# Sparse attention with a soft mixture behind it: the last tile's product in four parts, no filling products, the last copies and late loads in another order

## The chip, the cores and the metric

The kernel runs on one core of one Trainium2 chip. What counts is the device time of one execution in microseconds (us); the table below gives the median, the lowest and the highest of three runs of the kernel before, and the time of the one execution that was profiled.

## The reference

Two stages follow each other. The first is block-sparse attention: 4 batches, 8 heads, 768 positions, 64 columns per head, in blocks of 32 positions (24 blocks). A query block sees itself, its two neighbours, the first and the last block, and three sampled blocks; the first and last query blocks see everything. The second is a soft mixture of 8 experts with 4 slots each.

```python
def _attn_ref(q, k, v, sampled_blocks):
    scores = scale * np.matmul(q, k.transpose(0, 1, 3, 2))
    mask = np.abs(blk_i - blk_j) <= window
    mask = mask | (blk_i == 0) | (blk_j == 0) | (blk_i == n_blocks - 1) | (blk_j == n_blocks - 1)
    ...                                   # and the sampled blocks of each query block
    scores = np.where(mask, scores, -1000000000.0)
    attn = np.exp(scores - np.max(scores, axis=-1, keepdims=True))
    attn = attn / (np.sum(attn, axis=-1, keepdims=True) + 1e-09)
    return np.matmul(attn, v)

def _moe_ref(x, phi, w1, w2):             # x: 3072 x 512, phi: 512 x 32
    logits = x @ phi
    d = softmax of logits over the 3072 rows
    slot_input = (d.T @ x).reshape(E, S_per_e, D)
    for e in range(E):                    # w1[e]: 512 x 1024, w2[e]: 1024 x 512
        slot_out[e] = np.maximum(slot_input[e] @ w1[e], 0.0) @ w2[e]
    c = softmax of logits over the 32 slots
    return c @ slot_out.reshape(n_slots, D)
```

Everything is in float32. The softmax over all 3072 rows means that no expert can start before the last attention tile is done.

## The kernel before, in words

The attention is cut into 24 tiles of 128 rows, 6 per batch, named here (batch, tile): the last one is (3,5). A tile holds two units of two query blocks each, and heads come in two halves, r = 0 and 1. For a unit, PE forms the scores (`s`, line 538) from staged keys (`kst`), DVE takes their maxima (`nm`), ACT the exponentials (`p`), and DVE transposes them (`ptt`). POOL copies the value rows of the sampled blocks into staging buffers (`vrs`, line 482; six buffers, so that a buffer comes free when an older tile's product has read it). The product with the values (`av`, line 630, in `av_heads`) is 44 matrix products per half r of a tile, 42 for the last tile, which touches the border; PE runs each float32 product as two instructions and as many weight loads. DVE divides by the sums (`rs`, `x`, from `av_out`).

Four tiles make a group (`plan_group`). PE transposes each tile's `x` (`mxt`, line 826), ACT or DVE copies the result out (`xT`, line 375 or 377 in `evac`), PE forms the logits of the four tiles (`ml`, line 862); then come maximum (`nmx`), exponential (`dT`), a transposition (`md`, copied to `d`) and the sums `ms` = d.T @ x (line 917), which DVE adds to `sacc` and `ssum` (line 926). The last group, gi = 5, holds tiles (3,2) to (3,5). Its last tile is "split": half r = 0 goes to two banks of its own and is transposed before half r = 1 is done. Behind the last group stands a short serial stretch (`mr`, `mc`, `selw`, `psS`, `sT`), and then the experts: `pf` (line 1285, first weights) and `pso` (line 1293, second weights), which run over 64 weight pieces of 512 KB, and at last the combination (`po`, line 1388), copied out and stored.

The order of the work is not written out: each step is added to a plan with the engines that may do it, an estimated duration, what it depends on, the buffers that it takes, and a key. `Plan.run` simulates this with its own estimates and emits the instructions of every engine in the order that comes out. The key decides among steps that could start at about the same time; where a step may go to two engines, the simulation picks one. The engines then run their instructions in that fixed order and wait for each other by semaphores.

`Plan.run` also puts in filling products: where its simulation sees PE idle for more than 0.45 us late in the attention, it emits a few 128x128 products on the identity (`st`, by `warm`, line 397) whose result nobody reads.

SP issues the loads of weights. The first 23 pieces are loaded during the attention; then come 20 "late" ones in the order of `LORD`: digits are fresh buffers, "k" the freed key buffer (`kw`), "v" the freed value buffer `v1`, "o" two of the buffers that held transposed exponentials (`wx`). SP waits for each buffer in this order. The remaining 21 pieces go into buffers that the experts' products have read.

Of the kernel before, what the change touches and what calls it, by code (L numbers as in the profile page):

```python
# [21 lines left out]
P = 128  # L22
# [32 lines left out]

LORD = [0, 1, "k", "k", "k", 2, 3, 4, 5, "o", "o", "v", "v", "v", "v", 6, 7, 8, "v", "v"]
H1, HALF = 3, 4
# [24 lines left out]
class Plan:  # L82
# [14 lines left out]
    def run(self):  # L97
# [81 lines left out]
        todo = {e: [t for t in order if t.eng == e and t.pre] for e in at}  # L179
        pe_end = 0.0  # L180
        pe = []
        for t in order:
            q = todo[t.eng]
            while q and q[0].start <= t.start + 1.6:
                u = q.pop(0)
                u.vals = u.pre(u.eng)
            if t.eng == "PE":

                if (self.fill[0].fin < t.start < self.fill[2].fin and t.start - pe_end > 0.45
                        and sum(p == "s" and a < t.start and z > pe_end for p, _, a, z in spans) < SB):  # L190
                    self.fill[1](int((t.start - pe_end - 0.15) / 0.28))
                pe_end = t.fin
            i = t.f(t)
            if t.eng == "PE":
                last = next(i for i in reversed(self.tc.nc.cur_bb.bb.instructions) if i.engine == E_.PE)
                pe.append((t.fin, last.name))
            elif t.pace:

                name = [n for f, n in pe if f <= t.start - 1.5][-1]
                self.tc.add_manual_dep(i.ins, name, mybir.DependencyInfo(  # L200
                    mybir.DependencyClass.Sync, mybir.DependencyReason.DATA), reason="pace")
# [3 lines left out]
def attn_moe_kernel(ctx, tc, qT, kT, vfull, vtab, sampled, phi, w1, w2, out):  # L205
# [431 lines left out]

    def av_heads(T, rs_):

        vt, us = vtile[T.b], T.units  # L640
        one = len(us) == 1
        m = 64 * len(us)
        for n, c in enumerate((4, 5)):
            for r in rs_:
                for g, s_ in G2:
                    av_mm(T.av, 64 * r if one else 0, m, g, r, T.pt[r][s_, c, 0:m // BLK].rearrange("p j q -> p (j q)"),
                          vt[s_, :, VPOS((0, NB - 1)[n]), r, :], n == 0, False)
        for c in (1, 2):
            for w, u in enumerate(us):
                for r in rs_:  # L650
                    for g, s_ in G2:
                        av_mm(T.av, 64 * r if one else 64 * w, 64, g, r,
                              T.pt[r][s_, c, 2 * w:2 * w + 2].rearrange("p j q -> p (j q)"),
                              vt[s_, :, VPOS(2 * u.g + c), r, :], False, False)
        for n in range(NR + 1):
            for w, u in enumerate(us):
                for r in rs_:
                    for j in range(2):
# [14 lines left out]
    def plan_av(T, n):  # L673
# [12 lines left out]
        else:  # L686

            T.split = T is tiles.get((B - 1, NT - 1))

            def heads(t, r):  # L690
                if T.split and r == 0:
                    T.av = T.av0 = [psA.tile([P, 512], F32, tag="s", name="av", bufs=SB) for g in range(2)]
                elif r == 0 or T.split:
                    new_av(T)
                av_heads(T, (r,))
            if T.split:
                t_0 = add(lambda t: heads(t, 0), ("PE", 2.16), deps, n + 0.5, acq=[("s", use)] * 2, kind="av", mode="W3", ni=176)
                last = []
                t_a = add(lambda t: heads(t, 1), ("PE", 2.25), [t_0], n + 0.5, acq=[("av", last)], kind="av", mode="W3", ni=176)
                T.out = [add(lambda t, r=r: av_out(T, T.av if r else T.av0, 0, P, slice(r, r + 1)), ("DVE", 0.8 if r else 1.0),  # L700
# [115 lines left out]
    def plan_group(gi, Ts, last, final=False):  # L816
        st = Rec()
        t_xT, xT_use = [], []
        for n, T in Ts:
# [13 lines left out]
            if split:  # L833
                for h in range(2):
                    t_t = add(lambda t, h=h, turn=turn: turn(t, cs=range(h, 4, 2)), ("PE", 0.27), [T.out[h]], n + 2 + 0.01 * h, mode="F", ni=4,
                              acq=[] if h else [("pt", b_use)])
                    t_o = add(lambda t, h=h, out=out: out(t, cs=slice(h, 4, 2)), ("ACT", 0.4), [t_t], n + 2.1 + 0.01 * h,
                              acq=[] if h else [("xT", x_use)])
# [6 lines left out]
            t_t = add(turn, ("PE", 0.3), T.out, n + 2, acq=[("pt", b_use)], kind="xt", mode="F", ni=8)  # L845
            t_o = add(out, [("DVE", 0.69), ("ACT", 0.59)], [t_t], n + 2.1, acq=[("xT", x_use)], kind="xto")
            T.x_use.append(t_t)
# [111 lines left out]
        if split:  # L959
            t_lt.deps.append(t_dt)  # L960
            state.t_f = t_f = add(factor, ("ACT", 0.3), [t_do], k + 0.31)
            state.t_lo = t_lo
        use[2].append(t_do)
        t_s = add(sums, ("PE", 0.4), [t_do], k + 0.6, acq=[("pt", use[3])], kind="sum", mode="C", ni=16)
        d_use.append(t_s)
        state.t_s = t_s
        for _, T in Ts:
            T.x_use.append(t_s)
# [96 lines left out]
    for gi in range(6):  # L1065
        Ts = done[4 * gi:4 * gi + 4]
        t_m, k = plan_group(gi, Ts, Ts[-1][0])

# [94 lines left out]
    lp_use.extend([t_end, t_5])  # L1163
    t_z = add(f_zero, ("POOL", 1.1), [state.t_acc0.deps[0]], k, acq=[("xT", [t_end]), ("x", [t_end])])
    t_7 = [add(f_out, (e, 0.4), [t_end, t_z], k + 1.1) for e in ("DVE", "ACT")]
# [25 lines left out]
    ms.__enter__()  # L1191
    plan.fill = max(qks.items())[1], lambda n: warm(None, n), tiles[B - 1, NT - 1].t_av
    with tc.manual_schedule(engines={E_.SP}):
# [292 lines left out]
```

## Time and profile before

| | us |
|---|---|
| median of 3 runs | 309.68 |
| lowest and highest | 306.84 to 310.25 |
| the profiled execution, its own time | 307.04 |
| the span of its trace | 305.2 |
| around the span | 1.84 |
| attention until the first `pf` product | 252.0 |
| experts, combination, stores | 53.2 |

All places below are in us from the start of the span. The profiled execution is 2.64 us shorter than the median of the three runs. A trace shows for every instruction when it started and how long it took; where an engine stood idle in front of one, the releaser is named, or "issue" where it waited for nothing that the profile shows.

### The profile page before, as it was taken

Reading aid. Unit: us, or ns where it says so; the run is one execution under the profiler, and the core shown is the slowest. Engines: PE = TensorE matmul, PEld = TensorE weight load, DVE = VectorE, ACT = ScalarE, POOL = GpSimd, SP = SyncE. Lnnn points to the kernel's source line nnn. Section 1 sums busy time; section 2 is a strip of 40 time slices with the busy share of each in tenths; the row PEclk is TensorE's granted clock in tenths of the full one; section 3 lists DMA queues with packets and bytes.
Section 4 is the critical chain, followed back from the end, with each engine's and each line's share of the span. In section 5 each row is a group of like instructions: output and inputs, shape, how many; then the busy total and the mean of one; then the engine's idle time right before and its main releaser. Section 6 shows DMA issues by size and latency. Waiting matters only on the chain.

```text
span 305.2 us, 17541 instructions
## 1 busy us (share of the span) xinstructions
PE 275.6 (90%) x7147; PEld 191.6 (63%) x7147; DVE 219.3 (72%) x504; ACT 165.5 (54%) x522; POOL 177.4 (58%) x484
## 2 busy tenths in 40 slices
PE   7698999989999989999998999999797889999950
PEld 6158677666877765777675777767564652455640
DVE  4788988777999898898999689988882336012360
ACT  0877876842877584487577737676720041202450
POOL 2668788878758998394889759478454214000000
PEclk9869999999999999999999999999978899999996
DMA  7935676574576465264654625686686399999997
GB/s 244 400 116 160 177 198 193 143 203 102 165 207 182 132 170 139 64 171 120 170 151 127 175 55 154 154 222 178 212 258 227 107 382 375 413 410 406 313 305 256
DMA packets 31634, 63.61 MB, mean 208 GB/s; under 512 B 5313, under 2 KB 18754, under 8 KB 31554
## 3 DMA queue, kind: packets, MB, share of 16 engines
q1 hardware_dynamic: 31408, 62.37, 65.0%
q8 instruction: 56, 0.92, 1.3%
q14 instruction: 24, 0.20, 0.3%
q10 hardware_dynamic: 146, 0.13, 0.1%
HBM read 56.19 MB, written 6.29 MB: 205 GB/s over the span
## 4 chain that ended last, share of the span: by engine, by line
PE 70%; DVE 6%; DMA 5%; issue 4%; ACT 4%; POOL 4%; SPq 2%; POOLq 2%; ACTq 1%; DVEq 0%
PE av L630 28%; PE s L538 11%; PE avd L630 6%; PE pf L1285 5%; PE pso L1293 4%; PE mxt L826 4%; PE sd L735 3%; PE ms L917 2%; PE po L1388 2%; DMA ktile<-in_kT_dram 2%; PE ml L862 2%; POOL vrs L482 1%; POOLq L363 1%; ACT kst L464 1%; POOL kst L458 1%
## 5 line engine op out<-in xcount | busy, mean ns | idle before, releaser
L482 POOL COPY vrs<-v 128x260 f32 x264 | 95.7, 405 | 33.7 <-PE av L630 21.5
L558 ACT ACTIVATE p<-s,nm 128x256 f32<-128x256 f32 x176 | 72.6, 474 | 21.5 <-DVE nm L553 17.5
L630 PE MATMUL av<-v,ptt 64*64 64x130 f32 (+2 forms) x1728 | 76.1, 289 | 0.8 <-DVE x L625 0.6
L630 PEld LDWEIGHTS av<-v,ptt 64*64 64x64 f32 (+2 forms) x1728 | 51.3, 134 | 26.4 <-issue 15.0
L565 DVE STREAM_TRANSPOSE ptt<-p 128x512 f32<-128x512 f32 x88 | 58.6, 689 | 2.1 <-ACT p L558 2.0
L553 DVE TENSOR_REDUCE nm<-s 128x2 f32<-128x512 f32 x88 | 55.6, 676 | 2.3 <-PE s L538 2.0
L538 PE MATMUL s<-kst,q 64*32 64x256 f32 x1408 | 50.4, 387 | 4.7 <-ACT pd L766 2.8
L458 POOL COPY kst<-ktile 128x384 f32<-128x384 f32 x88 | 42.9, 507 | 13.3 <-PE s L538 13.3
L464 ACT ACTIVATE kst<-ktile 128x128 f32 x204 | 45.7, 300 | 8.7 <-PE s L538 5.7
L630 PE MATMUL av<-vrs,ptt 64*32 64x130 f32 x2112 | 45.8, 276 | 2.8 <-issue 2.8
L538 PEld LDWEIGHTS s<-kst,q 64*32 64x32 f32 x1408 | 30.0, 107 | 17.1 <-issue 4.1
L630 PEld LDWEIGHTS av<-vrs,ptt 64*32 64x32 f32 x2112 | 35.6, 105 | 4.2 <-issue 4.0
L766 ACT ACTIVATE pd<-sd,nb 128x384 f32<-128x384 f32 x32 | 16.6, 578 | 14.9 <-DVE nb L761 14.3
L375 ACT COPY xT<-mxt 128x512 f32<-128x512 f32 (+1 forms) x14 | 7.8, 555 | 30.1 <-PE mxt L826 29.7
L630 PE MATMUL avd<-v,ptd 64*64 64x130 f32 x768 | 23.1, 271 | 1.1 <-DVE x L625 0.9
L630 PEld LDWEIGHTS avd<-v,ptd 64*64 64x64 f32 x768 | 21.7, 132 | 2.6 <-PE s L538 1.3
L501 POOL TENSOR_SCALAR q<-q 128x256 f32<-128x256 f32 x33 | 13.2, 405 | 11.6 <-DMA q<-in_qT_dram 9.5
L753 DVE TENSOR_REDUCE nm<-sd 128x1 f32<-128x384 f32 x32 | 16.4, 545 | 3.7 <-PE sd L735 3.7
L735 PE MATMUL sd<-ktile,q 64*32 64x384 f32 x256 | 18.1, 531 | 1.0 <-ACT p L558 0.7
L770 DVE STREAM_TRANSPOSE ptd<-pd 128x384 f32<-128x384 f32 x32 | 16.3, 552 | 2.1 <-ACT pd L766 2.0
L625 DVE TENSOR_TENSOR x<-av,rs 128x512 f32<-128x512 f32 (+2 forms) x28 | 16.9, 605 | 1.1
L826 PE MATMUL mxt<-ident,x 128*128 128x128 f32 x96 | 16.1, 288 | 1.1 <-ACT lst L890 1.1
(128 smaller groups left out, 268.8 us busy)
## 6 DMA issues: line engine op xcount, KB each, us to landing
w<-in_w_dram SPq DMA_DIRECT2D x18, 512.0 KB, 8.1
v<-in_w_dram SPq DMA_DIRECT2D x12, 512.0 KB, 10.2
q<-in_qT_dram SPq DMA_DIRECT2D x47, 128.0 KB, 2.7
w<-in_w_dram SPq DMA_DIRECT2D x44, 128.0 KB, 3.5
out_dram<-ob SPq DMA_DIRECT2D x19, 256.0 KB, 3.2
ktile<-in_kT_dram SPq DMA_DIRECT2D x48, 96.0 KB, 3.0
v<-in_w_dram SPq DMA_DIRECT2D x24, 128.0 KB, 3.4
kw<-in_w_dram SPq DMA_DIRECT2D x6, 512.0 KB, 6.6
```

What stands on the lines that cost most here:

```text
L458: POOL.tensor_copy(out=st[:, :, w:w + 96], in_=kv[:, :, (i - 1) * BLK:(i + 2) * BLK])
L464: ACT.activation(out=st[:, :, o:o + BLK], in_=src, func=AF.Copy, scale=1.0)
L482: POOL.tensor_copy(out=st[:, :, j:j + 1, :], in_=vf[:, :, ds(t.vals[j], 1), :])
L538: PE.matmul(u.s[r][32 * p:32 * p + 32, j, :], lhsT=u.q[s_, p, j, :], rhs=kd[j][0][s_, p, :], start=True, stop=True)
L553: DVE.tensor_reduce(out=u.nm[r], in_=u.s[r], axis=AX.X, op=ALU.max, negate=True)
L558: ACT.activation(out=u.p[r][:, j, :], in_=u.s[r][:, j, :], func=AF.Exp, bias=u.nm[r][:, j:j + 1], scale=1.0)
L565: DVE.transpose(out=T.pt[r][:, :, 2 * w:2 * w + 2, :].rearrange("p k j q -> p j k q"), in_=u.p[r].rearrange("p j (k q) -> p j k q", k=8))
L625: DVE.tensor_tensor(out=x, in0=a[:, :, :, 0:D], in1=rs[lo:hi].unsqueeze(3).to_broadcast([hi - lo, 2, 2 * n, D]), op=ALU.mult)
L630: PE.matmul(av[:, r * 2 * D1:(r + 1) * 2 * D1].rearrange("p (a d) -> p a d", a=2), lhsT=lhsT, rhs=rhs, start=start, stop=stop)
L735: PE.matmul(u.s[r][k][32 * p:32 * p + 32, :], lhsT=T.dq.q[s_, p, j, :], rhs=kt[s_, p, 384 * k:384 * (k + 1)], start=True, stop=True)
L766: ACT.activation(out=u.p[r][k], in_=u.s[r][k], func=AF.Exp, bias=u.nb[r], scale=1.0)
L826: PE.transpose(T.px[:, c, :], T.x[:, c * P:(c + 1) * P], ident)
```

## The change

It has six parts.

1. No filling products: the code in `Plan.run` that emits them is gone, and the line that switched it on.
2. The last tile's product, two steps before (half r = 0, then half r = 1), is four: part 0 (all of r = 0 that needs only the first unit's staged values), part 2 (what r = 1 takes from the value buffer itself), part 1 (the rest of r = 0), part 3 (the rest of r = 1), in the order 0, 2, 1, 3.
3. In the last group the copies `xT` may only go to ACT.
4. The split tile's two half copies get a late key (n + 9).
5. For the group before the last (gi = 4) the copy `d` and the sums `ms` get an earlier key (minus 8). The zeroing of `sT` gets a later one (k + 20); POOL's order stays as it was.
6. `LORD`: the second "o" stands behind the first four "v".

```diff
-LORD = [0, 1, "k", "k", "k", 2, 3, 4, 5, "o", "o", "v", "v", "v", "v", 6, 7, 8, "v", "v"]
+LORD = [0, 1, "k", "k", "k", 2, 3, 4, 5, "o", "v", "v", "v", "v", "o", 6, 7, 8, "v", "v"]
...
-            if t.eng == "PE":
-
-                if (self.fill[0].fin < t.start < self.fill[2].fin and t.start - pe_end > 0.45
-                        and sum(p == "s" and a < t.start and z > pe_end for p, _, a, z in spans) < SB):
-                    self.fill[1](int((t.start - pe_end - 0.15) / 0.28))
-                pe_end = t.fin
             i = t.f(t)
...
-    def av_heads(T, rs_):
+    def av_heads(T, rs_, part=None):
...
-        for n, c in enumerate((4, 5)):
+        ws = {None: [(0, 1)] * 4, 0: [(0, 1), (0,), (0,), (0,)], 1: [(), (1,), (1,), (1,)], 2: [()] * 4, 3: [(0, 1)] * 4}[part]
+        first = part in (None, 0, 2)
+        for n, c in enumerate((4, 5) if first else ()):
...
-        for c in (1, 2):
+        for c in (1, 2) if first else ():
...
         for n in range(NR + 1):
             for w, u in enumerate(us):
+                if w not in ws[n]:
+                    continue
...
             if T.split:
-                t_0 = add(lambda t: heads(t, 0), ("PE", 2.16), deps, n + 0.5, acq=[("s", use)] * 2, kind="av", mode="W3", ni=176)
-                last = []
-                t_a = add(lambda t: heads(t, 1), ("PE", 2.25), [t_0], n + 0.5, acq=[("av", last)], kind="av", mode="W3", ni=176)
+                last, tn, ts = [], T.turned, T.staged
+                t_0 = add(lambda t: heads(t, 0, 0), ("PE", 1.6), [tn[0], tn[2], ts[0], ts[1], t_v[T.b]], n + 0.5, acq=[("s", use)] * 2, kind="av", mode="W3", ni=128)
+                t_1 = add(lambda t: heads(t, 1, 2), ("PE", 0.65), [t_0] + tn, n + 0.5, acq=[("av", last)], kind="av", mode="W6", ni=48)
+                t_0 = add(lambda t: heads(t, 0, 1), ("PE", 0.6), [t_1] + ts, n + 0.5, kind="av", mode="33", ni=48)
+                t_a = add(lambda t: heads(t, 1, 3), ("PE", 1.55), [t_0], n + 0.5, kind="av", mode="33", ni=128)
...
-                    t_o = add(lambda t, h=h, out=out: out(t, cs=slice(h, 4, 2)), ("ACT", 0.4), [t_t], n + 2.1 + 0.01 * h,
+                    t_o = add(lambda t, h=h, out=out: out(t, cs=slice(h, 4, 2)), ("ACT", 0.4), [t_t], n + 9 + 0.01 * h,
...
-            t_o = add(out, [("DVE", 0.69), ("ACT", 0.59)], [t_t], n + 2.1, acq=[("xT", x_use)], kind="xto")
+            t_o = add(out, [("DVE", 0.69), ("ACT", 0.59)][final:], [t_t], n + 2.1, acq=[("xT", x_use)], kind="xto")
...
+        if gi == 4:
+            t_do.key -= 8
...
+        if gi == 4:
+            t_s.key -= 8
...
-        t_m, k = plan_group(gi, Ts, Ts[-1][0])
+        t_m, k = plan_group(gi, Ts, Ts[-1][0], gi == 5)
...
-    t_z = add(f_zero, ("POOL", 1.1), [state.t_acc0.deps[0]], k, acq=[("xT", [t_end]), ("x", [t_end])])
+    t_z = add(f_zero, ("POOL", 1.1), [state.t_acc0.deps[0]], k + 20, acq=[("xT", [t_end]), ("x", [t_end])])
...
-    plan.fill = max(qks.items())[1], lambda n: warm(None, n), tiles[B - 1, NT - 1].t_av
```

Since the plan sets the order, the diff does not show what moves. Up to the scores of the last unit every engine keeps its order. The first place is PE between the second half of tile (3,4) and the last tile (3,5). Before, with `vrs` the staged values, `v` the value buffer, `st` the filling products:

```order
L630 MATMUL av<-vrs_102,ptt 32x130 x2
L917 MATMUL ms<-x,d 32x512 x4
L826 MATMUL mxt<-ident,x 128x128 x4
L397 MATMUL st<-ident 128x128 x4
L630 MATMUL av<-v_69,ptt 128x130 x4
L630 MATMUL av<-v_69,ptt 64x130 x8
L630 MATMUL av<-v_69,ptt 32x130 x6
L630 MATMUL av<-vrs_103,ptt 32x130 x2
```

The same place in the changed kernel, on PE, from the end of tile (3,4) to the start of part 1:

```order
L623 MATMUL av<-vrs_102,ptt 32x130 x2
L623 MATMUL av<-v_69,ptt 128x130 x4
L623 MATMUL av<-v_69,ptt 64x130 x8
L623 MATMUL av<-v_69,ptt 32x130 x6
L623 MATMUL av<-vrs_103,ptt 32x130 x2
L623 MATMUL av<-vrs_104,ptt 32x130 x2
L623 MATMUL av<-vrs_103,ptt 32x130 x2
L623 MATMUL av<-vrs_104,ptt 32x130 x2
L623 MATMUL av<-vrs_103,ptt 32x130 x2
L623 MATMUL av<-vrs_104,ptt 32x130 x2
L830 MATMUL mxt<-ident,x 128x128 x4
L623 MATMUL av<-v_69,ptt 128x130 x4
```

The sums `ms` now stand ahead of the transposition of (3,2), that of (3,3) between the two halves of tile (3,4), and that of (3,4) behind part 0 of the last tile; the filling products, one in front of tile (3,4) and four here, are gone. On DVE, behind `ms`, the addition to `sacc` now stands ahead of the last unit's maxima `nm`.

The second place is DVE behind the last tile's second half, where `x` is finished; `mxt` is the transposed tile (3,4). Before:

```order
L623 TENSOR_SCALAR rs<-av 128x4
L624 RECIPROCAL rs<-rs 128x4
L625 TENSOR_TENSOR x<-av,rs 128x2x128
L377 COPY xT<-mxt 128x512
L875 TENSOR_REDUCE nmx<-ml 128x1
```

The same place of the changed kernel on DVE:

```order
L616 TENSOR_SCALAR rs<-av 128x4
L617 RECIPROCAL rs<-rs 128x4
L618 TENSOR_TENSOR x<-av,rs 128x2x128
L879 TENSOR_REDUCE nmx<-ml 128x1
L881 TENSOR_TENSOR nmx<-nmx 128x1
```

The copy of tile (3,4) has gone to ACT, where it stands ahead of the two half copies of the last tile.

The third place is SP's late loads. Before:

```order
L232 DMA w_7109<-in_w_dram 128x1024
L232 DMA w_7111<-in_w_dram 128x1024
L232 DMA wx<-in_w_dram 128x1024 x2
L232 DMA v_69<-in_w_dram 128x1024 x4
L232 DMA w_7119<-in_w_dram 128x1024
```

SP in the changed kernel, the same loads:

```order
L225 DMA w_7102<-in_w_dram 128x1024
L225 DMA w_7104<-in_w_dram 128x1024
L225 DMA wx<-in_w_dram 128x1024
L225 DMA v_69<-in_w_dram 128x1024 x4
L225 DMA wx<-in_w_dram 128x1024
```

The four loads into the value buffer no longer stand behind the second `wx`, whose buffer the last tile's half r = 0 reads.

## Rows read from the trace of the kernel before

**Rows 1.** The page: its head, its busy times, and queue 8, which carries instructions.

```profile
span 305.2 us, 17541 instructions
...
PE 275.6 (90%) x7147; PEld 191.6 (63%) x7147; DVE 219.3 (72%) x504; ACT 165.5 (54%) x522; POOL 177.4 (58%) x484
...
q8 instruction: 56, 0.92, 1.3%
```

**Rows 2.** Chain that ended last, 219 to 253: start, us, what.

```profile
219.14 1.88 issue
...
224.59 0.67 PE mxt L826 x4
...
225.48 4.75 PE av L630 x174
230.23 0.98 PE ms L917 x5
231.21 2.27 issue
233.48 1.05 PE ms L917 x3
234.53 0.59 PE mxt L826 x4
235.12 1.71 PE st L397 x8
236.84 3.07 PE av L630 x83
...
240.50 2.45 PE av L630 x83
...
243.38 0.42 DVE x L625
...
244.55 0.64 PE ml L862 x12
245.19 0.37 PE mxt L826 x2
...
248.48 1.07 PE ms L917 x8
...
252.00 1.05 PE pf L1285 x5
```

**Rows 3.** Windows: length; busy (count) PE, PEld, DVE, ACT, POOL; clock; DMA share; GB/s

```profile
219.50:231.90 12.40, 10.19 (x255) 6.27 (x255) 7.65 (x23) 3.08 (x10) 6.28 (x18) 0.86 0.80 261
...
224.80:235.00 10.20, 7.93 (x195) 5.05 (x194) 4.71 (x12) 2.06 (x5) 5.23 (x15) 1.00 0.79 264
235.00:238.40 3.40, 3.40 (x26) 2.94 (x28) 2.23 (x9) 0.58 (x1) 1.64 (x4) 0.50 0.04 12
...
235.30:240.40 5.10, 5.10 (x96) 4.12 (x94) 2.31 (x12) 0.44 (x1) 1.69 (x4) 0.70 0.00 0
...
252.00:288.00 36.00, 36.00 (x434) 18.38 (x438) 10.36 (x32) 8.24 (x18) 3.75 (x6) 1.00 1.01 385
```

**Rows 4.** Timeline of DVE behind the last product.

```profile
243.72 0.68 DVE L377 COPY xT<-mxt 128x512 f32<-128x512 f32 x1
```

**Rows 5.** Timeline of POOL's last staging copies and of SP's late loads.

```profile
229.81 2.14 POOL L482 COPY vrs<-v 128x260 f32 x6 [3.57 <-PE av L630]
...
230.76 9.58 SPq L232 DMA_DIRECT2D wx<-in_w_dram  x2
240.44 2.20 SPq L232 DMA_DIRECT2D v<-in_w_dram  x4
```

**Rows 6.** The last weight pieces (`ptd`): loads, use, and time to landing.

```profile
L1293 PEld LDWEIGHTS pso<-ptd,hT x24: 110/110/110, 286.9 to 288.0; 128*32 128x32 f32 x24
...
L232 SPq DMA_DIRECT2D ptd<-in_w_dram x3: 328/328/328, 272.5 to 275.1; - x3
...
DMA to landing us min/median/max: 10.1/10.1/10.1
```

More of the change, by code (lines that the diff above doesn't have):

```diff
@@ L179, in run @@
         todo = {e: [t for t in order if t.eng == e and t.pre] for e in at}
-        pe_end = 0.0
         pe = []
@@ L688, in plan_av, with heads @@
             T.split = T is tiles.get((B - 1, NT - 1))
[L690 to L693, printed above, removed]
+            def heads(t, r, part=None):
+                if T.split and part == 0:
+                    T.av0 = [psA.tile([P, 512], F32, tag="s", name="av", bufs=SB) for g in range(2)]
+                elif part == 2:
                     new_av(T)
-                av_heads(T, (r,))
-            if T.split:
-                t_0 = add(lambda t: heads(t, 0), ("PE", 2.16), deps, n + 0.5, acq=[("s", use)] * 2, kind="av", mode="W3", ni=176)
-                last = []
-                t_a = add(lambda t: heads(t, 1), ("PE", 2.25), [t_0], n + 0.5, acq=[("av", last)], kind="av", mode="W3", ni=176)
+                    T.av1 = T.av
+                elif not T.split and r == 0:
+                    new_av(T)
+                if T.split:
+                    T.av = T.av1 if r else T.av0
+                av_heads(T, (r,), part)
+            if T.split:
+                last, tn, ts = [], T.turned, T.staged
[3 more added lines that the diff above has]
+                t_a = add(lambda t: heads(t, 1, 3), ("PE", 1.55), [t_0], n + 0.5, kind="av", mode="33", ni=128)
                 T.out = [add(lambda t, r=r: av_out(T, T.av if r else T.av0, 0, P, slice(r, r + 1)), ("DVE", 0.8 if r else 1.0),
```

## The prediction

> **What bounds the kernel now.** I read the page first: PE is busy for 90% of the span [rows 1], so time is won where PE stands or works for nothing. Then the chain that ended last, around the end of the attention [rows 2]. The reader is to see three things in it. PE stops twice for "issue", that is for no semaphore: 1.88 us at 219.14 and 2.27 us at 231.21. The eight filling products at 235.12 stand on the chain with 1.71 us. And from 243.38 the chain leaves PE for DVE, which first makes `x` and then copies tile (3,4) [rows 4] before PE gets its logits at 244.55.
>
> Then the windows [rows 3]. Between the two stops lie 255 products and 255 weight loads, 510 instructions. Queue 8 brought 56 packets of code for 14,294 PE instructions [rows 1], 255 for each packet, so the stops are two packets apart: I take them for PE waiting for its next packet, and note that the DMA share in this stretch is 0.80. Some 1.5 us after the second stop the clock is granted at 0.50 (1.2 GHz), from 235.0 to 238.4. In 235.3 to 240.4 the DMA moves nothing, because SP stands at the second `wx` [rows 5]. From 252.0 on PE is busy for 36.0 of 36 us with the DMA share at 1.01 [rows 3]: the experts.
>
> **The change part by part.** Parts 1, 2 and 5 move work around the second stop, so I count from its end, 233.48.
>
> *Ahead of it.* Before, PE went from 224.59 to 231.21 through one `mxt`, one filling row, both halves of tile (3,4) (4.75) and five of the eight `ms`. The boundary of a code packet lies at a place in PE's instruction stream, 187 products after 224.59 (4 + 2 + 176 + 5). In the new order these 187 are 8 `ms`, 4 `mxt`, 88 `av`, 4 `mxt` and 83 of the 88 of the second half. They take 1.07 + 0.67 + 2.37 + 0.59 + 2.24 = 6.94 us where 6.62 stood [rows 2], so PE comes to the boundary at 231.5, 0.3 later, which the stop swallows as long as the packet comes when it came. What is moved ahead is therefore free. `ms` needs `d`, whose copy DVE now makes ahead of `x` of tile (3,3); that shift of 0.3 us reaches nobody, since `mxt` of (3,3) comes a half product later. Behind `ms` on DVE waits the addition, and behind it the last maxima, which start some 2 us later than before; the last exponential then also waits on ACT behind the copy of (3,3). I get the last transposition at 231.0, and part 2, the first that needs it, starts behind the stop. Were there no stop, it would still be there 2 us early.
>
> *Behind it.* Before, from 233.48: `ms` 1.05, `mxt` 0.59, filling 1.71, half 3.07, `mxt` 0.59, half 2.45, ending at 242.95, 9.5 us [rows 2]. Gone or moved ahead are `ms`, one `mxt` and the filling, 3.35. Added are 5 products of tile (3,4), 0.13. The 1.2 GHz stretch of 3.4 us lay on filling for half its length and on the product for 1.56 us, in which the first half lost 3.07 - 2.45 = 0.62. Now all 3.4 us lie on the product: 0.62 x 3.4 / 1.56 = 1.35, so 0.73 more. Net 3.35 - 0.13 - 0.73 = 2.5 us; the product ends at 240.45.
>
> The Trainium skill, "TensorE: Matmul & The Clock Gate", section "What's actually happening", says that the throttled state is the default and that activity releases the throttle, which speaks against taking filling products away. By that rule the clock could stay low longer here; the sum for it is the third rival.
>
> The four parts cost nothing themselves: 84 products before and after. They hide the staging. POOL's last six copies take 2.14 us [rows 5] and wait for reads by the second half of tile (3,4), all of which lie ahead of the packet boundary, so they run during the stop; without one, part 0 (60 of 168 instructions, about 1.9 us), `mxt` and part 2 (together about 1.6) would cover them. What part 0 of r = 0 delays is `x` of r = 0: it is about 1 us of DVE behind part 1 (an estimate: twice the `x` row's 0.42 and small steps), beside part 3 of 60 instructions, about 1.2. If that cover fell, at most 1 us.
>
> *The copy* (parts 3 and 4). Before, from the end of the product, 242.95, to the last `mxt`, 245.19, went 2.24 us: `x` until 243.80, the copy of (3,4) behind it, then 12 `ml`. ACT makes that copy while the product runs. What is late next is `x` (0.85) or PE's own row of two `mxt` and 12 `ml` (0.37 + 0.64): 1.05 with a step between. Saved: 1.15. From there to `pf` nothing changes, 6.8 us.
>
> *Loads* (part 6). The four `v` loads wait for POOL's last copy, not for r = 0. They leave at about 234.5 behind `wx`, where before they left at 240.44. The piece in front of `wx` now waits for the last product of (3,4), so it goes some 3 us later; together 3 MB are let go in 2 us. Of the 5.1 idle us of the DMA about 4 are used. That is not on the chain by itself, but it is the cover for the rest: the last weights were issued at 275.1, landed 10.1 later at 285.2 and were used at 286.9 [rows 6], a slack of 1.7 us with the DMA full. Without part 6 a gain of 3.6 would run into it. With it, loads and PE both come earlier by about the same.
>
> *Sum.* 2.5 + 1.15 = 3.6 us off the chain at `pf`, 252.0 to 248.4; the experts and the stores follow at the same distance. The profiled execution, 307.04, becomes 303.4. The median of three runs is 2.64 above it, for a reason that the trace cannot show; I keep that distance: 309.68 - 3.6 = **306.1**, 1.2% less. A change of 1% is about what a measurement of this kernel can tell from none.
>
> Bounds: the packet may come 0.6 us later, if its wait counts from PE's crossing of the boundary before (a half us later now): gain 3.0. If the low stretch shrinks with the idle, up to 1.35 more.
>
> **The rivals.**
>
> *No stop.* I take it that the packet is asked for when PE enters the one before; whether it is late hangs on what the DMA holds then. If the shift of half a microsecond lets it come in time, the product starts at 231.5 + 0.13 instead of 233.6, and with no stop there is no low stretch: 2.0 + 1.35 more, gain 7.0, 302.7 for the median. For it: the boundary one packet earlier, about 227, was crossed without a stop. Against: the loads in flight in front of the packet do not move, and DMA ran at 264 GB/s with share 0.79 [rows 3]. The Trainium skill, "Runtime: NRT & Kernel Launch", section "Instruction fetch mechanics", says that the crossing of such a boundary is mostly hidden; by that the stops would not come back, but this trace shows two within 13 us [rows 2].
>
> *A new stop in the last product.* This one ends slower. The next boundary falls at the sixth product of part 3, reached about 239.4. The packet is asked for at 233.5, just when six loads, 3.1 MB, are let go. If it has to wait behind them all, at 264 GB/s [rows 3] they take 12 us; it would be there at about 246, PE would stand for 6.6 us and run slow for another stretch, 1.35: 306.1 + 8 = 314. It decides from a stop of 2.3 us plus that stretch, then the gain is eaten. Against it: the request goes out shortly before the loads.
>
> *The clock stays down.* Without filling, another low stretch on the serial part or on `pf` costs 1.35, two 2.7: 307.5 to 308.8, no change that could be told. Against: PE is not busier with filling than with the product, and between 243 and 252, with idle in between, no such stretch was seen.
>
> *It isn't on the chain.* If `pf` comes earlier but the weights don't, the gain stops at the slack of 1.7: 308.0.
>
> **How the numbers follow.** Forecast 306.1: 0.58, itself 304.9 to 307.5 by its bounds and the scatter of runs. No stop, 302.7: 0.14. Clock or weights, 307.5 to 308.8: 0.20. New stop, above 310: 0.08. The range takes in the second rival's lower edge and the third: 302.6 to 309.0. Faster by over 1% means under 306.6: most of the forecast (0.38) and all of "no stop", 0.52. Within 1%: 0.20 of the forecast, 0.18 of clock and weights, 0.01 of the new stop, 0.39. Slower: 0.09.
>
> **What would show it.** Right: no `st` behind 200; an "issue" stop of some 2 us at the end of tile (3,4), around 231.5, not in `ms`; the last product at about 240.5; `ml` behind it without a wait for DVE; `pf` at 248.4; `v` loads at 234.5 and no idle DMA of 5 us. Wrong: a stop in part 3, a low clock behind 241, or `pf` waiting for weights.

## The result and the profile after

The changed kernel takes 302.85 us (median of 22 runs, 299.6 to 305.67); the kernel before, run beside it, 306.73 (median of 22 runs). The ratio is 0.9897, 95% interval 0.9869 to 0.9924, that is 2.3 to 4.0 us less. Ratios, here and below, leave out runs that lie more than 1.5% above the fastest of their kernel; medians do not. The forecast was 3.6 us less, and a time of 306.1 by way of the first three runs' median; the 22 runs of before lie 3 us below that. The profiled execution of the changed kernel took 301.3 us, its span is 299.5.

The page answers [rows 1]: 3.8 us of PE's busy time are gone, with ten matrix instructions, and the code still comes in 56 packets.

```profile
PE 271.8 (91%) x7137; PEld 190.3 (64%) x7137; DVE 219.2 (73%) x503; ACT 166.1 (55%) x523; POOL 178.4 (60%) x484
```

The chain of the changed kernel from 219 to 253 (start, us, what) answers [rows 2]:

```profile
220.85 0.51 issue
...
226.92 0.86 issue
...
229.26 2.33 PE av L623 x83
231.59 0.47 issue
...
235.35 2.96 PE av L623 x104
...
238.40 0.44 PE mxt L830 x2
238.84 0.57 PE ml L866 x12
...
246.21 7.05 PE pf L1292 x61
```

Three things are to be seen. `pf` starts at 246.21, 5.8 us earlier than at 252.00 in [rows 2]. PE now stops three times for "issue", one code packet apart, and each time shortly: 1.84 us in all, where there were two stops with 4.15. The last of them stands where it was forecast, behind the 83rd instruction of the second half of tile (3,4), at 231.59. (The number behind an x counts matrix instructions, two to each product of the kernel; "the 47th product" of a row, below, counts these too.) And nothing between the last product (ends 238.31) and `ml` waits for DVE.

A window of the changed kernel (columns as in [rows 3]) shows the clock at 1.00, which is 2.4 GHz, over the whole last product:

```profile
231.00:238.40 7.40, 6.84 (x215) 5.17 (x203) 4.45 (x17) 0.59 (x1) 5.47 (x14) 1.00 0.63 201
```

SP's late loads in the changed kernel's timeline answer [rows 5]: the four `v` loads leave at 233.45, not at 240.44.

```profile
233.45 2.49 SPq L225 DMA_DIRECT2D v<-in_w_dram  x4
```

From the start of `pf` to the end of the span lie 299.5 - 246.21 = 53.3 us; before, 305.2 - 252.0 = 53.2. So the whole difference of the two traces is made ahead of `pf`. But 5.8 us there and 3.2 by the ratio do not agree: a part of it belongs to these two executions and not to the kernels. That, and which part of the change brings what, is what the experiments are for.

### The profile page after: what moved, and what is told of

The parts are those of the page before. It is cut to its first block, busy times and chain, and to the rows that moved or that the text cites. A ratio compares the mean times of both kernels' runs of the same rounds, so it can differ in the third digit from the quotient of the medians.

```text
span 299.5 us, 17519 instructions
## 1 busy us (share of the span) xinstructions
PE 271.8 (91%) x7137; PEld 190.3 (64%) x7137; DVE 219.2 (73%) x503; ACT 166.1 (55%) x523; POOL 178.4 (60%) x484
## 4 chain that ended last, share of the span: by engine, by line
PE 62%; POOL 7%; DMA 6%; issue 6%; POOLq 5%; DVE 4%; ACT 4%; ACTq 1%; SPq 1%; DVEq 0%
PE av L623 25%; PE s L531 9%; PE avd L623 6%; PE pf L1292 5%; PE pso L1300 4%; POOLq L356 4%; PE mxt L830 4%; DMA q<-in_qT_dram 3%; POOL vrs L475 3%; PE sd L739 3%; POOL kst L451 2%; PE ms L921 2%; DMA ktile<-in_kT_dram 2%; PE po L1395 2%; PE ml L866 2%
## 5 line engine op out<-in xcount | busy, mean ns | idle before, releaser
L531 PE MATMUL s<-kst,q 64*32 64x256 f32 x1408 | 49.1, 380 | 4.9 <-ACT pd L770 2.8
L623 PE MATMUL av<-vrs,ptt 64*32 64x130 f32 x2112 | 48.3, 278 | 3.4 <-issue 3.3
L531 PEld LDWEIGHTS s<-kst,q 64*32 64x32 f32 x1408 | 30.7, 106 | 16.1 <-POOL kst L459 3.4
L623 PEld LDWEIGHTS av<-vrs,ptt 64*32 64x32 f32 x2112 | 36.8, 106 | 6.4 <-issue 6.2
L368 ACT COPY xT<-mxt 128x512 f32<-128x512 f32 (+1 forms) x15 | 8.4, 558 | 20.6 <-PE mxt L830 20.2
L739 PE MATMUL sd<-ktile,q 64*32 64x384 f32 x256 | 16.0, 490 | 1.6 <-ACT p L551 1.6
## 6 DMA issues: line engine op xcount, KB each, us to landing
v<-in_w_dram SPq DMA_DIRECT2D x12, 512.0 KB, 10.4
```

The source lines that it names most:

```text
L531: PE.matmul(u.s[r][32 * p:32 * p + 32, j, :], lhsT=u.q[s_, p, j, :], rhs=kd[j][0][s_, p, :], start=True, stop=True)
L623: PE.matmul(av[:, r * 2 * D1:(r + 1) * 2 * D1].rearrange("p (a d) -> p a d", a=2), lhsT=lhsT, rhs=rhs, start=start, stop=stop)
L739: PE.matmul(u.s[r][k][32 * p:32 * p + 32, :], lhsT=T.dq.q[s_, p, j, :], rhs=kt[s_, p, 384 * k:384 * (k + 1)], start=True, stop=True)
```

## The experiments

My theory: what is taken off behind the stop, and the copy, make the gain; the loads are cover; the four parts are free. Its rivals: the loads, the order in part 5 or the shorter stops are the gain. The kernels ran in three groups of four, each group beside runs of the kernel before on the same chip: parts 1 and 3 alone and parts 2 and 6 undone in the first, on a chip on which the changed kernel itself was not run again, the other eight on another.

### The changed kernel and the kernel before, once more

> The changed kernel itself, unaltered, on the chip of the other runs of this call. Expected 0.987 to 0.993 against before. For its trace: the stops stand at the same products as in its first trace (47 and 83), since the places are fixed by the instruction count, but their lengths differ, by up to 1 us each, since they hang on how far the loads are; rival: the lengths are the kernel's own and repeat within 0.1 us.

> The kernel before itself, as a control: ratio 1.000 with an interval that holds it, which shows how far a ratio of these runs can be off. For its trace: stops after the 53rd product of the first half of (3,2) plus one transposition row, and after the fifth of the eight sums `ms`, as in its first trace; if the second stop is well under 2 us there is no 1.2 GHz stretch behind it and `pf` starts 2 to 4 us earlier counted from the start of the last scores; if it is 2 us or more the stretch is there again.

The changed kernel: 0.9915 (0.9883 to 0.9946), 302.62 against 305.25 us. The kernel before against itself: 0.9991 (0.9951 to 1.0032). The two comparisons of the changed kernel with before give the gain as 1.03% and 0.85%, and a ratio of these runs can be off by some 0.4%. Here is the second trace of the kernel before, its chain from 219 on:

```profile
221.37 1.02 PE s L538 x32
...
222.98 0.24 PE st L397 x2
...
223.26 1.92 PE av L630 x53
225.18 0.87 issue
...
229.29 0.98 PE ms L917 x5
230.27 0.42 issue
230.69 1.05 PE ms L917 x3
...
232.33 0.89 PE st L397 x8
233.22 2.36 PE av L630 x83
...
236.17 2.46 PE av L630 x82
...
247.68 7.93 PE pf L1285 x72
```

The stop stands behind the fifth `ms`, as in [rows 2], but it is 0.42 us long and not 2.27. The boundary ahead of it, which the first trace crossed freely, now shows 0.87. No stretch at 1.2 GHz follows, and the eight filling products take 0.89, not 1.71. A window over them (columns as in [rows 3]) shows the clock at 1.00:

```profile
232.00:234.00 2.00, 2.00 (x28) 1.76 (x29) 1.93 (x8) 0.58 (x1) 0.68 (x2) 1.00 0.75 293
```

The second trace of the changed kernel has its stops at the same products as the first one, with other lengths: nothing to speak of at the 47th product, 0.47 at the 83rd. So the place of a stop belongs to the kernel, its length to the execution, and the 1.2 GHz stretch that I counted on was in one of the two executions that were traced.

These two executions are alike enough for a sum. From the first of the last scores to `pf`, before took 247.68 - 221.37 = 26.31 us and the changed kernel 245.96 - 223.06 = 22.90: 3.4 us less. The rows of its second trace:

```profile
223.06 1.02 PE s L531 x32
224.08 0.99 PE ms L921 x8
...
231.35 0.47 issue
231.82 2.70 PE av L623 x65
...
235.11 2.96 PE av L623 x104
...
245.96 7.93 PE pf L1292 x72
```

- Filling: 0.24 + 0.89 and a step of 0.05, 1.2 less.
- `ms`: 0.98 + 1.05 where a stop cut it, 0.99 in one piece: 1.0 less.
- Stops: 0.87 + 0.42 against 0.05 + 0.47: 0.8 less, by chance of these two.
- From the product's end to `pf`: 247.68 - 238.63 = 9.05 against 245.96 - 238.07 = 7.89: 1.2 less.
- The last tile's product: 2.36 + 2.46 = 4.82 against 2.70 + 2.96 less the five products of tile (3,4) (0.13), 5.53: 0.7 more.

Together, unrounded, 3.4 us.

### Part 1 alone: no filling products

```diff
-                if (self.fill[0].fin < t.start < self.fill[2].fin and t.start - pe_end > 0.45
+                if (self.fill[0].fin < t.start < self.fill[2].fin and t.start - pe_end > 1e9
```

> The kernel before with part 1 alone: no filling products, every other instruction where it was. Theory: the 1.71 us of the eight filling products leave the chain, and if the slow-clock stretch of 3.4 us comes all the same, its whole length falls on the last tile's product, 0.73 us back. `pf` starts about 1.0 us earlier, the time is about 0.3% less (ratio 0.994 to 1.000), and the stretch of 1.2 GHz is still there. Rival 1, the filling kept the clock up: a longer stretch at 1.2 GHz, 1.35 us or more for each, ratio 1.000 or above. Rival 2, the filling stood in front of a wait: an idle of about 1.7 us ahead of the last tile's product, released by POOL or DVE, and no gain.

Measured 0.9955 (0.9915 to 0.9995), 1.4 us less, in the theory's range. In its trace the last two stops are 1.41 and 0.58 us, and the profile page's clock row shows no fall behind them, with no filling in place. In this execution neither rival is seen: the clock did not fall without filling, and no wait took its place. The second stop stands behind the seventh `ms` and not the fifth, since two filling products ahead of it are gone: the boundary counts instructions. My own theory was wrong on the 1.2 GHz stretch here too.

### Parts 3 and 4: the copies

```diff
-            t_o = add(out, [("DVE", 0.69), ("ACT", 0.59)], [t_t], n + 2.1, acq=[("xT", x_use)], kind="xto")
+            t_o = add(out, [("DVE", 0.69), ("ACT", 0.59)][final:], [t_t], n + 2.1, acq=[("xT", x_use)], kind="xto")
```

Part 3 alone:

> The kernel before with part 3 alone: the last group's copies of transposed tiles only on ACT. Theory: from the end of the last product to the last transposition 1.05 to 1.3 us instead of 2.24, `pf` about 1.0 us earlier, ratio about 0.996 to 0.997. Rival, ACT becomes late: the two half copies of the last tile queue behind the copy of tile (3,4) on ACT, the logits wait for ACT instead of DVE, and the gain is under 0.3 us (ratio 0.999 to 1.001).

It brought no gain, rather a small loss: 1.0038 (1.0007 to 1.0069). The chain shows the rival:

```profile
239.93 2.36 PE av L630 x83
...
242.69 0.87 ACT xT L375 x2
...
243.60 0.64 PE ml L862 x12
```

Behind the last product PE's `ml` waits for two copies of ACT. From the product's end, 242.29, to `pf` at 251.05 go 8.76 us, 0.3 less than before. Then with part 4, the late key of the two half copies (and the later zeroing of `sT`, without which the plan has no order):

```diff
-                    t_o = add(lambda t, h=h, out=out: out(t, cs=slice(h, 4, 2)), ("ACT", 0.4), [t_t], n + 2.1 + 0.01 * h,
+                    t_o = add(lambda t, h=h, out=out: out(t, cs=slice(h, 4, 2)), ("ACT", 0.4), [t_t], n + 9 + 0.01 * h,
```

> The kernel before with parts 3 and 4 together (and the later key of the zeroing of `sT`, which the late copies need): the copy of tile (3,4) on ACT, ahead of the last tile's half copies. Theory: with part 3 alone the logits waited for ACT's two copies in the wrong order; in this order the time from the last product's end to `pf` is 7.9 to 8.1 us, as in the changed kernel, against 9.05 before, ratio 0.996 to 0.998. Rival, the copies are worth nothing that reaches the end: 1.000 to 1.004, as with part 3 alone.

Measured 0.9937 (0.9899 to 0.9976), 1.9 us less. In its chain the product ends at 237.46 and `pf` starts at 245.30:

```profile
235.00 2.46 PE av L630 x82
...
245.30 7.93 PE pf L1285 x72
```

That is 7.84 us, what the changed kernel needs, and 1.2 less than in the second trace of before. The ratio is a little better than the 0.996 to 0.998 that I gave; the interval holds the copy's 1.2 us (0.996), and what else the 1.9 may hold is not shown. Parts 3 and 4 are one edit: the copy pays only if the half copies stand behind it on ACT.

### Part 2 undone: the last product in two parts

```diff
-                t_0 = add(lambda t: heads(t, 0, 0), ("PE", 1.6), [tn[0], tn[2], ts[0], ts[1], t_v[T.b]], n + 0.5, acq=[("s", use)] * 2, kind="av", mode="W3", ni=128)
-                t_1 = add(lambda t: heads(t, 1, 2), ("PE", 0.65), [t_0] + tn, n + 0.5, acq=[("av", last)], kind="av", mode="W6", ni=48)
-                t_0 = add(lambda t: heads(t, 0, 1), ("PE", 0.6), [t_1] + ts, n + 0.5, kind="av", mode="33", ni=48)
-                t_a = add(lambda t: heads(t, 1, 3), ("PE", 1.55), [t_0], n + 0.5, kind="av", mode="33", ni=128)
+                t_0 = add(lambda t: (heads(t, 0, 0), heads(t, 0, 1)), ("PE", 2.16), deps, n + 0.5, acq=[("s", use)] * 2, kind="av", mode="W3", ni=176)
+                t_a = add(lambda t: (heads(t, 1, 2), heads(t, 1, 3)), ("PE", 2.25), [t_0], n + 0.5, acq=[("av", last)], kind="av", mode="W3", ni=176)
```

> The changed kernel without part 2 (the last tile's product in two parts as before). Theory: the four parts hold no time of their own, since the last staging copies of POOL end at about the time at which the first 60 products are through; within 0.3% of the changed kernel, 0.987 to 0.993 against before. Rival, the four parts hide the staging or the transposition of tile (3,4): PE waits 0.5 to 1.0 us for POOL or for the copy behind the stop, and the ratio is 0.993 or above.

Measured 1.0063 (1.0014 to 1.0112): without part 2 the change loses all of its gain, and by this interval 0.1% or more beyond. The theory that the four parts hold nothing of their own falls. Its trace shows why. The plan now puts the transposition of tile (3,4) ahead of the whole last product, where `x` of (3,4) is not ready:

```profile
233.99 1.01 issue
235.00 0.44 PE av L623 x5
...
236.74 1.09 PE mxt L828 x4
237.82 7.36 PE av L623 x165
```

PE stops for code, runs the last five products of (3,4), waits 1.30 us for DVE, and then runs the product in 7.36 us. A window of this trace shows the clock at 0.50 (1.2 GHz):

```profile
236.60:240.00 3.40, 3.26 (x29) 2.39 (x29) 1.63 (x6) 0.58 (x1) 2.51 (x6) 0.50 0.94 251
```

Is it the place of the transposition, or the two parts? One row of the changed kernel was moved, the transposition of (3,4), from behind part 0 to ahead of it; every other row of every engine stayed:

```diff
+                T.t_first = t_0
                 t_1 = add(lambda t: heads(t, 1, 2), ("PE", 0.65), [t_0] + tn, n + 0.5, acq=[("av", last)], kind="av", mode="W6", ni=48)
...
+            if T is tiles[B - 1, NT - 2]:
+                tiles[B - 1, NT - 1].t_first.deps.append(t_t)
```

> The changed kernel with one row moved: the transposition of tile (3,4) stands ahead of part 0 of the last tile's product instead of behind it; nothing else moves on any engine. New theory, what the four parts (and the filling before) are worth is the place of this transposition: in its new place PE waits for DVE's `x` of (3,4), about 1.3 us, right behind a stop for code, and the clock then falls to 1.2 GHz over the last product in most executions, 2.5 us; the time is that of the run with two parts, ratio 1.000 to 1.008 against before, and the trace shows `mxt` waiting for DVE. Rival, the old theory: the four parts as such hide the staging by POOL, and the place of the transposition costs nothing: 0.990 to 0.994.

Measured 1.0015 (0.9970 to 1.0060), against 0.9897 and 0.9915 for the changed kernel, whose intervals end below 0.9970: this one row is worth about 1%, 3 us. Its chain and one window:

```profile
230.39 1.29 issue
231.68 0.44 PE av L623 x5
...
233.42 0.94 PE mxt L831 x4
234.36 6.47 PE av L623 x162
```

```profile
233.80:237.10 3.30, 3.30 (x43) 2.37 (x45) 1.11 (x3) 0.59 (x1) 2.27 (x6) 0.51 0.97 254
```

The same wait of 1.30 us (231.68 + 0.44 to 233.42), and 3.3 us at 1.2 GHz behind it. The staging is not in it: no wait for POOL stands in either trace. What part 2 does is to put 60 matrix instructions, those that need nothing new, between the end of (3,4) and its transposition. In the kernel before, the first half of the last tile did that.

### Part 6 undone: the loads

```diff
-LORD = [0, 1, "k", "k", "k", 2, 3, 4, 5, "o", "v", "v", "v", "v", "o", 6, 7, 8, "v", "v"]
+LORD = [0, 1, "k", "k", "k", 2, 3, 4, 5, "o", "o", "v", "v", "v", "v", 6, 7, 8, "v", "v"]
```

> The changed kernel without part 6 (the late loads in the order of before). Theory, the loads are cover and no gain of their own: `pf` starts where it does in the changed kernel, but the second load into `wx` waits for the last tile's half r = 0 (about 238.5) and the four loads into the value buffer behind it leave at about 238.6 instead of 233.5; the DMA stands idle for about 3 us, the slack of the last weights is 1.5, so the end comes 1.0 to 2.0 us later than in the changed kernel: ratio against before 0.993 to 0.997. Rival, the slack carries it: as the changed kernel, 0.990. Rival, the loads are the gain: 0.998 or above.

Measured 0.9946 (0.9906 to 0.9986), where theory had 0.993 to 0.997. The interval overlaps those of the changed kernel, so the ratio alone does not tell the two apart; the trace does. `pf` starts at 246.51, as in the changed kernel, but 302.1 - 246.51 = 55.6 us lie behind it instead of 53.3. SP's queue and the chain of this run:

```profile
238.25 2.83 SPq L225 DMA_DIRECT2D v<-in_w_dram  x4
```

```profile
262.71 10.87 DMA v<-in_w_dram
```

The `v` loads leave 4.8 us later, and the chain of the end runs through their landing. In this execution, then, the loads are cover, as forecast. With the order of before, the two kernels above with parts 1 or 3 and 4 alone needed no such cover (53.4 and 53.3 us behind `pf`, 299.4 - 246.03 and 298.6 - 245.30). I take it that this is because in the changed kernel the last tile's half r = 0, which `wx` waits for, ends behind part 1 and not after the product's first 84 matrix instructions. The trace with parts 3 and 4 alone bears it out: that half ends at 234.41 there, the `v` loads leave at 234.93, 10.4 us ahead of `pf`, and in the run shown here only 8.3 ahead.

### Part 5 undone: the keys of the group before the last

```diff
-            t_do.key -= 8
+            t_do.key -= 0
...
-            t_s.key -= 8
+            t_s.key -= 0
```

> The changed kernel without part 5's earlier keys: the sums `ms` of the group before the last stand behind tile (3,4)'s product again and two transpositions one place later each. Theory: the work is the same and only the stop's share of it moves; behind the stop stand 0.6 us more (one transposition row), so 0.2% at most: 0.987 to 0.995 against before. Rival, part 5 clears DVE for the last unit: PE waits for the last transposed exponentials or for `x` in front of part 1 or 2, 0.5 us or more, and the ratio is above 0.995.

Measured 0.9934 (0.9892 to 0.9975), beside 0.9915 for the changed kernel on the same chip: not to be told apart. The rival falls, PE waits for nobody but code there. Its stop in `ms` cut that row once more, behind the seventh of eight.

### What the stops hang on

Half a code packet (64 matrix instructions, 64 weight loads) put in at the start of the program, and then a whole one:

```diff
         for j in range(n):
             PE.matmul(st[:, 0, 0:P], lhsT=ident, rhs=ident, start=True, stop=True)
+        for j in range(32):
+            PE.matmul(st[0:32, 1, 0:32], lhsT=ident[0:32, 0:32], rhs=ident[0:32, 0:32], start=True, stop=True)
```

> The changed kernel with 32 more tiny products (32x32 on the identity, 64 matrix instructions and as many weight loads) at its very start, whose result nobody reads. Theory, PE's stops lie at the ends of code packets, counted from the first instruction: they move 64 matrix instructions ahead in the work, that is from 47 products into the first half of tile (3,4) to about 27 of the last unit's 32 scores, and from 83 products into its second half to about 19. Their sum stays between 1 and 4 us and the time within 0.6% of the changed kernel (0.984 to 0.996 against before). Rival, the stops hang on the place in the work or on the loads in flight: they stay behind the 47th and the 83rd product.

Measured 0.9853 (0.9775 to 0.9930), within the range named, with single runs from 296.1 to 307.7; the trace is of the fastest of them. Its chain:

```profile
224.22 4.91 PE av L625 x147
...
229.71 2.96 PE av L625 x103
...
233.20 0.57 PE ml L868 x12
233.76 0.47 issue
```

Nothing stops at the 47th and 83rd product any more. A stop appears behind 12 `ml`: from the end of part 0, half a packet behind the old place, 4 `mxt`, 108 products, 2 `mxt` and 12 `ml` are 126 matrix instructions, with their weight loads about a packet. At the other two places that I had named no stop shows, so the sum of 1 to 4 us was wrong. PE waited 0.46 us for DVE's `d` in front of `ms` instead.

With 64 added products (128 matrix instructions) in place of 32:

> The changed kernel with 64 more tiny products at its very start instead of 32: 128 matrix instructions and 128 weight loads, one whole code packet. Theory, the ends of the packets decide where PE can stop: shifted by a whole packet they fall on the same products as in the changed kernel, so stops are seen again near the 47th product of tile (3,4)'s first half and near the 83rd of its second half (within two products), and the time goes back to the changed kernel's, 0.985 to 0.996 against before, slower than with half a packet on the same footing by 0 to 1%. Rival, any extra products at the start do what half a packet did: no stop between 214 and 232, and 0.980 to 0.988.

```profile
231.07 1.83 PE av L625 x47
232.90 0.41 issue
...
234.78 2.33 PE av L625 x83
237.11 1.57 issue
```

The stops are back at the 47th and the 83rd product, to the instruction. That settles the place. The ratio, 1.0004 (0.9969 to 1.0038), is beyond the range that I gave and 0.9% above the changed kernel's. The first scores start at 13.60 instead of 12.1 to 12.3 (with half the added products at 12.03, no later), so about 1.4 us (0.5%) may be the added products themselves, and the rest I leave open. The trace shown is of one of the longest executions, so only its places are used.

The last one asks why the packets are late. The four `v` loads stand at the head of the late loads, so that SP waits there and the DMA is quiet:

```diff
-LORD = [0, 1, "k", "k", "k", 2, 3, 4, 5, "o", "v", "v", "v", "v", "o", 6, 7, 8, "v", "v"]
+LORD = ["v", "v", "v", "v", 0, 1, "k", "k", "k", 2, 3, 4, 5, "o", "o", 6, 7, 8, "v", "v"]
```

> The changed kernel with the four loads into the value buffer at the head of the late loads, so that SP stands until POOL's last staging copy and no weights are loaded from about 213 to 233. Theory, the packets come late because they stand behind loads: the stops between 214 and 233 vanish or shrink to 0.3 us in all (1.84 in the changed kernel), and PE comes to the last tile's product some 1.5 us sooner after the stop-free work before; but 41 weight pieces are left to load from 233.4 on at some 1.3 us each, the last lands at about 288 and the time is 4 to 7 us longer than the changed kernel's (ratio 1.003 to 1.013 against before). Rival, packets are late whatever else is loaded: stops of 0.5 to 2 us at the same places.

Windows and chain of this run:

```profile
214.00:230.00 16.00, 15.18 (x454) 10.66 (x449) 14.84 (x40) 8.18 (x30) 9.10 (x26) 1.00 0.02 5
```

```profile
226.20 4.67 PE av L623 x146
...
242.31 3.37 PE pf L1292 x29
245.68 10.37 DMA w<-in_w_dram
```

With a DMA share of 0.02 both halves of (3,4) and part 0 run through without a stop, and `pf` starts at 242.31, 3.9 us earlier than in the changed kernel's first trace. Not all of that is the stops: the last 32 `ml` ahead of this stretch start at 213.31 here and at 215.30 and 215.60 in the changed kernel's two traces, so about 2 us were there before the loads were held back. From these `ml` to `pf` it takes 29.0 us against 30.9 and 30.4, 1.4 to 1.9 less, with a wait of 0.82 for DVE's `d` in front of `ms` that the changed kernel did not have. Soon after it starts, `pf` waits for weights; the ratio is 1.0157 (1.0075 to 1.0238), a little beyond the 1.003 to 1.013 that I gave. So the stops hang on loads in flight: none shows in the one trace without them. But a busy DMA alone does not make one: with half a packet shifted, the share was 0.87 to 1.00 from 220 to 226, and PE crossed a boundary there without a stop that shows.

What decides is when the packet comes, and queue 8 tells that. Here is its row for 230.5 to 233.5 of the first trace of before, around the stop of 2.27:

```profile
q8 instruction: 1, 0.02, 2.1%
```

One packet, and 2.1% of 16 engines' 3.0 us are the 1.0 us that it took; in smaller windows it runs from 231.10 to 232.11. PE goes on at 233.48, 1.4 us behind its end. In the changed kernel's first trace the packets end at 219.93, 226.27 and 230.71, and the three stops at 221.36, 227.78 and 232.06. For every code stop that a chain shows between 218 and 240, in all fourteen traces, the distance is 1.2 to 1.5 us: a stop lasts until its packet is there. With the DMA quiet the packets started 0.7 to 1.0 us after PE had crossed the boundary before; those of the changed kernel's second and third stop started 4.0 and 1.9 us after. Why one starts later than another among the loads stays open.

## Why the prediction was right, and where its terms were off

The forecast of 3.6 us less stands against 3.2 (2.3 to 4.0) in the first comparison and 2.6 (1.6 to 3.6) in the second. The time itself, 302.85, lies only 0.25 above the lower end of the range and next to the 302.7 of "no stop". That is luck on both sides: the median of three runs that I added to was 3 us too high, and the lower end lies just below the time of a rival that did not come true. The place of the stop, the early `v` loads, the free `ml`, the 53 us behind `pf` and the copy's 1.15 us (measured 1.16) came as the prediction said. Four terms did not.

**Behind it, 2.5 us.** I took the second stop's 1.2 GHz stretch as a property of the kernel: 1.71 for the filling, and 0.73 to be paid back by the product. The second trace of before has no such stretch. In an execution without it the term is 1.05 + 0.59 + 0.89 - 0.13 = 2.4 without the payback.

**The four parts cost nothing themselves.** They cost 0.7 us in this pair: 168 matrix instructions before and after, but 5.53 us instead of 4.82 (2.28 + 1.25 + 1.71 = 5.24 in the trace without part 5, 0.4 more; part 0 alone, which I put at 1.9 us, took 2.28 there). By luck this is the size of the payback that did not come, so what is left of the term is 1.7. Ahead of the stop I had called all moves free, since the stop would swallow them; with stops this short they count: filling (0.3) and stop time (0.8, chance) came off, a transposition (0.6) was added. 1.7 + 0.5 + 1.2 for the copies is 3.4.

**What they hide.** I said the staging, and that if the cover fell it would be 1 us at most. The staging was never waited for. They hide DVE's work on `x` of (3,4), 1.30 us, and with it the fall of the clock: some 3 us by the measured ratios. I listed `mxt` (3,4) behind part 0 in the order of the change and did not ask what it would cost in front.

**An issue stop of some 2 us.** It was 0.47, and 0.47 again. Of the rivals, "no stop" was half right: the stops' lengths are not fixed by the kernel. But that gives no 7 us: in the second trace of before the two stops behind the last scores are 1.3 us together, and with the quiet DMA the changed kernel gained 1.4 to 1.9 us up to `pf`. Without a stop PE also came too early for `d`, a wait (0.46 and 0.82 us) that my sum for this rival did not have. "A new stop in the last product" and "the clock stays down" did not come in the changed kernel's traces. That filling holds the clock up is nowhere seen: in the first trace of before it fell with the filling in place. "It isn't on the chain" is what happens without part 6.

Part 1 (0.45%) and parts 3 with 4 (0.63%) measured alone, each known to some 0.4%, make 1.1% together, as much as the whole change. If they add, parts 2 and 6 only keep it from being lost, and part 5 does nothing that these runs show. Whether parts 1, 3 and 4 without the rest would do as well was not run. Nor is it settled whether the new order shortens the stops: behind the last scores they sum to 1.3 to 2.3 us in the five traces with the order of before and to 0.5 to 1.9 in the five with the changed order up to the last product.

## What to carry to other kernels

Profile the same kernel twice before a stop or a slow-clock stretch goes into a sum: its place repeated to the instruction here, its length did not. When an engine's order is changed, ask of each row not what it costs but what it waits for in its new place; a transposition of 0.6 us cost 3 us in the wrong one, and the key change nothing that could be measured. And test the parts of an edit together with what they lean on: the copy alone gained nothing, with the late keys behind it 0.6%.

## What the runs showed of the hardware

PE's stops stand at the ends of its code packets, counted in instructions; they were 0 to 2.3 us long with the DMA busy and gone at a DMA share of 0.02, and PE went on 1.2 to 1.5 us behind the end of the packet on queue 8. Granted clock: it fell to 1.2 GHz for 3.3 us or more behind a stop of 1.88 us, one of 2.27, and two idles of 1.29 and 1.30 (1.01 and 1.30) with five products between them; it did not fall behind single stops of 1.57, 1.51, 1.41 and 1.33. That it fell behind two idles close together, each shorter than stops behind which it did not fall, I had not expected; two traces show it, and no run shows that the second idle is what did it. The window of the first trace of before, right behind its stop of 1.88:

```profile
221.00:224.40 3.40, 3.38 (x68) 1.61 (x68) 2.25 (x9) 0.00 (x0) 2.26 (x7) 0.55 0.84 271
```

And `ms`, eight instructions of 512 columns, takes 0.99 to 1.07 us in one piece at the full clock and up to 2.03 with a stop in it, beside the stop itself (1.91 in the trace with part 3 alone, where no stop shows in it).
